# Block-diagonal centroid products, weight joins through PSUM and a re-ordered opening in a clustered-attention and MLP kernel

## The chip, the cores and the metric

The kernel runs on one core of a Trainium2 chip. A core has a matmul engine (TensorE, called PE in the profile; its weight loads are shown apart as PEld), a vector engine (DVE), an activation engine (ACT), a general engine (POOL) and a queue that issues most of the transfers (SP). Each of them executes its own instructions strictly in program order and waits on semaphores for the others. PE writes only to PSUM, in banks of 512 float32 values per partition; DVE and ACT read PSUM and SBUF. The metric is the device time of one execution in microseconds (us).

## The reference

For each of 4 batches and 8 heads, queries and keys (768 of them, 64 wide) are assigned to the nearest of 16 centroids of the head; a query attends only to keys of its own cluster. The result, laid out as 768 rows of 512, is mixed along the sequence by two thin matrices and goes through an MLP.

```python
q_assign = np.argmax(np.einsum('bhsd,hcd->bhsc', q_n, c_n), axis=-1)   # k_assign alike
mask = q_assign[:, :, :, None] == k_assign[:, :, None, :]
scores = np.where(mask, scale * np.matmul(q, k.transpose(0, 1, 3, 2)), -1000000000.0)
attn = np.exp(scores - np.max(scores, axis=-1, keepdims=True))
x = np.matmul(attn / (np.sum(attn, -1, keepdims=True) + 1e-09), v)     # heads side by side: 768 x 512
xt = x.transpose(0, 2, 1)
u = x + (xt @ U @ V).transpose(0, 2, 1)
out = u + np.maximum(u @ w_ch1, 0.0) @ w_ch2
```

Here q and k are the tensors themselves in the scores and q_n, k_n, c_n their normalised forms in the assignment. U, V and the two MLP weights arrive as float64.

## The kernel before

**Items.** The attention works on 16 items, each a pair of heads of one batch (index `i`, 4 items per batch). An item is loaded transposed into `R` (L303): queries on partitions 0-63, keys on 64-127, four blocks of 384 columns, one for each half of the sequence and each head. `sims` (L309) multiplies it with the turned centroids `cT` on PE, `largest` (L320) and `clusters` (L333) find the first largest of 16 on DVE (five operations) and leave a one-hot matrix `oh`. The one-hot rows are turned and scaled into rows 64-95 of the operand `X1`, so that the score product itself carries the mask: by `turn_clusters` (L399) for item 0, by `clusters_T` and `place_clusters` (transfers) for the others.

**Precision.** An operand is kept as a rounded part (`X1`, written by `split_hi`, ACT) and the rest (`X2`, written by `split_lo`, L360: POOL for the first two items, DVE for the others); transfers (`place_...`, queue SP) lay the two parts out in the buffer `arena` so that one pair of matmuls (L447, L449) gives the full score.

**Maxima, scores, values.** `rowmax` (L415) makes 24 products per item and half-row (L423), and DVE reduces each (L425) into `m2`; `rowmax_T` (L427) takes the larger of two halves (L430, `m`), and `rowmax_place` (L432) turns that on PE (L435), negates it on ACT (L437) and sends it by a transfer on ACT's queue to row 96 of `X2`. `scores` (L441) makes a tile `st`, ACT exponentiates it to `pr` (L452), `weights` (L455) adds the tiles up to `T` on POOL (a few on DVE), and `values` (L464) multiplies with V (L470, `o_ps`). `sums`, `sums_T` and `normalise` divide. `mix_u`, `mix_sum` and `mix_v` do the mixing for a batch.

**Weights.** They come as pairs of 32-bit words and are turned into float32 on the way: `upper` (L139, ACT) scales the high word into `rw_g`, and `join` (L147) puts shifted high bits, sign and low bits together in three DVE operations on the SBUF tile `rw_t` (L154, L156, L159), each issued as a stage of its own at its own time. `load_weights` (L165) then splits the result for four groups `g` of 8 pieces (ACT, and POOL or DVE); group 0 and three `mix` pieces lie inside the attention, group 1 around its end, groups 2 and 3 in the MLP. The MLP (`gemm1`, `gemm2`, L570 to L594) follows, all on PE, starting with `turn_u` (L561).

**What sets the order.** `at(time, fn, ...)` collects calls with a due time in units of one score tile (12 per item); the list is sorted by time and called in that order, and `keep_order` pins each engine to it. The due times are in `times`, `spots`, `start`, `mix` and `pieces`. All short-lived PSUM tiles come from one pool of four buffers (`work`, L124): a new tile waits until the readers of the tile four places earlier are done.

Of the kernel before, what the change touches and what calls it, by code (L numbers as in the profile page):

```python
# [29 lines left out]
F32 = mybir.dt.float32  # L30
F32R = mybir.dt.float32r
# [28 lines left out]
    "load0":           ( -34.7, -34.39, -42.04,   None,   None,  -24.6),  # L60
    "load1":           (-26.06, -29.53, -32.88,   None,   None, -24.08),
    "sims":            ( -25.1, -28.71, -28.37,   None,   None, -21.52),
    "clusters_T":      (-19.61, -19.11, -17.87,   None, -12.09, -14.53),
    "place_clusters":  (-18.66, -16.14, -16.18,   None, -10.54, -11.62),
    "split_hi0":       (-29.08, -30.53, -24.36,   None,   None, -21.63),
    "split_lo0":       (-24.34, -23.65, -24.04,   None,   None, -17.46),
    "split_hi1":       (-23.95,  -23.8, -24.91,   None,   None, -19.95),
    "split_lo1":       (-23.57, -19.94, -23.55,   None,   None, -17.17),
    "place_keys_hi":   (-20.26, -23.52, -23.41,   None,   None, -17.07),
    "place_keys_lo":   (-19.99, -19.89, -21.05,   None,   None, -16.87),  # L70
    "place_queries":   (-17.03, -15.79, -18.99,   None,   None, -16.31),
    "place_ones":      (-14.59, -12.48, -10.02,   None,   None, -19.67),
    "load_v":          (-19.47,  -3.83,  -5.91,   None, -22.04, -10.41),
    "rowmax":          (-14.88, -14.94,  -14.8, -13.95,  -8.61,  -11.6),
    "rowmax_T":        ( -3.08,  -3.31,  -3.73,  -2.67,  -0.09,  -1.59),
    "rowmax_place":    ( -2.26,  -2.27,   -2.6,    1.6,   2.02,  -0.01),
    "scores":          (     0,  -0.97,  -0.58,  -0.47,  -1.09,   0.95),
    "weights":         (  1.23,   0.08,   0.52,   2.09,   3.85,    1.7),
    "values":          (  1.27,   1.37,   0.22,   1.05,   3.05,   1.39),
    "sums":            ( 14.65,  14.41,  13.18,  14.01,  15.28,  15.65),  # L80
    "sums_T":          ( 16.16,  16.37,  14.51,  15.86,  17.12,   16.3),
    "normalise0":      ( 18.83,  16.88,  15.76,  22.66,  20.81,  21.01),
    "normalise1":      ( 21.68,  17.59,  15.29,  26.53,  23.24,  23.11),
    "largest":         (-23.05, -22.36, -20.51,   None,   None, -21.05),
    "clusters":        ( -21.3, -22.24, -19.87,   None,   None, -18.24),
# [3 lines left out]
spots = [0.61, 0.02, 1.8, 2.25, 1.26, 2.09, 2.97, 3, 3.58, 3.81, 4.64, 5.05]  # L89
# [13 lines left out]
def clustered_attention_moe(ctx: ExitStack, tc: tile.TileContext, qk, v, cen, moe_U, moe_V, w1, w2, out):  # L103
# [43 lines left out]
    def join(rw, g, t, k):  # L147
# [4 lines left out]
        if k == 0:  # L152
# [12 lines left out]
    def load_weights(g, step, stage):  # L165
# [39 lines left out]
    ident_b = one.tile([P, P], BF16, name="ident_b")  # L205
    make_identity(nc, ident_b)
    rank = one.tile([P, C], F32, name="rank")
    for c in range(C):
        nc.gpsimd.memset(rank[:, c:c + 1], float(C - c))
    osc = one.tile([P, 1], F32, name="osc")  # L210
    nc.gpsimd.memset(osc[0:64], 1.0)
    nc.gpsimd.memset(osc[64:128], BIG)
    obi = one.tile([P, 1], F32, name="obi")
    nc.gpsimd.memset(obi, 0.0)
# [6 lines left out]
    for g in range(4):
        for r in range(3):
            nc.gpsimd.tensor_copy(rep[32 * g:32 * g + 32, 32 * r:32 * r + 32],
                                  ident[32 * g:32 * g + 32, 32 * g:32 * g + 32])
# [17 lines left out]
    def turn_centroids(p):  # L244
        ps = work("ps_c")
        nc.tensor.transpose(ps[:, 0:P], c_sb[:, p], ident)
        for h in range(2):
            dst, src = (x.rearrange("p (s u c) -> p s u c", s=4, u=2)[:, :, h] for x in (cT[:, p, h], ps[:, 0:P]))
            nc.scalar.copy(dst, src)
# [20 lines left out]
    def load_mix(k, stage):  # L270
# [7 lines left out]
        elif stage < 5:  # L278
            parts["mix", k] = join(*parts["mix", k], stage - 2)
# [17 lines left out]
    live = {}  # L297

# [10 lines left out]
    def sims(i):  # L309

        ps = work("ps_sim")
        for h in range(2):
            for s in range(4):
                r = slice(64 * (s // 2), 64 * (s // 2) + 64)
                nc.tensor.matmul(ps[32 * s:32 * s + 32, 0:HS], cT[r, i % NP, h, 32 * s:32 * s + 32],  # L315
                                 live["R", i][r, 2 * h + s % 2, :], start=(h == 0), stop=(h == 1))
# [424 lines left out]
```

## Time and profile before

| | |
|---|---|
| three runs | 1041.81, 1037.4, 1041.7 us (median 1041.7) |
| the profiled execution | 1038.17 us; its span from first to last instruction is 1036.3 us, so 1.9 us lie around it |
| busy over the span | PE 999.4, PEld 793.5, DVE 533.2, ACT 350.1, POOL 342.6 us |
| opening, before the first score | 0 to 35.7 us |
| attention | 35.7 to about 479 us |
| MLP | about 479 to 1036.3 us |

A row of the time line gives start, duration, engine, line of the kernel, operation, output and inputs with their shapes, the number of instructions merged in the row, and in square brackets how long the engine had stood idle before it and what ended that. A row of the windows gives for a stretch of time the busy time of each engine, then the TensorE clock that was granted (1.00 is full), the share of the DMA engines and GB/s.

### The profile page before, as it was taken

The page shows a single profiled execution, that of the slowest core. Times are in us where ns is not written, and L with a number is a line of the kernel's source. Part 1 is how long each engine was busy: PE and PEld are TensorE (multiplying, and loading weights), DVE is VectorE, ACT ScalarE, POOL GpSimd, SP SyncE. Part 2 cuts the span into 40 slices and gives each one's busy share as a digit, 9 for nine tenths or more (in the row PEclk, how much of TensorE's full clock was granted, in tenths as well). Part 3 has the DMA queues.
Part 4 walks back from the last instruction along what each step waited for, and adds up shares of the span by engine and source line. Part 5 has one row for each costly group of instructions (what it writes and reads, how often), then busy time and mean ns, then how long its engine had stood idle before and what let it go on. Part 6 is the DMA issues. An engine that isn't in the chain of part 4 may idle for free.

```text
span 1036.3 us, 13926 instructions
## 1 busy us (share of the span) xinstructions
PE 999.4 (96%) x5496; PEld 793.5 (77%) x5496; DVE 533.2 (51%) x928; ACT 350.1 (34%) x572; POOL 342.6 (33%) x228
## 2 busy tenths in 40 slices
PE   4889999999999999989999999999999999999998
PEld 2566666666666666656889999999999999999997
DVE  4698898888898768798773121121121221211211
ACT  4344555555555544455332111111111111111110
POOL 4455667788578857754231000000000000000000
PEclk8799999999999999989999999999999999999999
DMA  5746453665565544243442001010010010100000
GB/s 147 192 119 150 132 150 93 198 158 144 128 196 140 140 97 129 71 129 103 151 164 80 1 1 61 1 38 24 1 62 1 1 61 1 61 1 1 31 1 31
DMA packets 28688, 87.73 MB, mean 85 GB/s; under 512 B 4880, under 2 KB 9488, under 8 KB 28112
## 3 DMA queue, kind: packets, MB, share of 16 engines
q1 hardware_dynamic: 28240, 86.76, 29.8%
q8 instruction: 43, 0.70, 0.3%
q14 instruction: 21, 0.17, 0.1%
q10 hardware_dynamic: 384, 0.10, 0.0%
HBM read 42.99 MB, written 12.58 MB: 54 GB/s over the span
## 4 chain that ended last, share of the span: by engine, by line
PE 87%; DVE 4%; ACT 1%; DMA 1%; issue 1%; ACTq 0%; DVEq 0%; SPq 0%
PE o_ps L470 12%; PE ps_h L576 9%; PE ps_h L578 9%; PE ps_h L577 9%; PE y L594 9%; PE y L593 9%; PE y L592 8%; PE ps_max L423 6%; PE st L447 6%; PE st L449 5%; PE ps_sim L315 1%; PE ps_sum L482 1%; DVE m L425 1%; PE ps_oT L503 1%; PE ps_uT L565 1%
## 5 line engine op out<-in xcount | busy, mean ns | idle before, releaser
L582 DVE SCALAR_TENSOR_TENSOR hl<-ps_h,hh 128x384 fp32r<-128x384 f32 x128 | 71.3, 557 | 349.6 <-ACT hh L581 349.6
L462 POOL TENSOR_TENSOR T<-T,pr 128x768 f32<-128x768 f32 x120 | 229.6, 1913 | 59.6 <-DVE T L462 26.7
L425 DVE TENSOR_REDUCE m<-ps_max 128x1 f32<-128x384 f32 x384 | 195.0, 547 | 58.7 <-PE ps_max L423 57.4
L581 ACT ACTIVATE hh<-ps_h 128x384 fp32r<-128x384 f32 x128 | 62.9, 492 | 375.5 <-PE ps_h L578 375.4
L452 ACT ACTIVATE pr<-st 128x768 f32<-128x768 f32 x192 | 155.3, 813 | 86.2 <-PE st L449 70.9
L423 PE MATMUL ps_max<-arena 128*128 128x384 f32 x384 | 125.3, 381 | 11.3 <-DVE oh L342 4.1
L470 PE MATMUL o_ps<-pr,vt 128*64 128x384 f32 x768 | 131.5, 492 | 0.0
L593 PE MATMUL y<-w2l,hh 128*128 128x512 f32 x288 | 113.6, 394 | 0.0
L447 PE MATMUL st<-arena 128*128 128x384 f32 x384 | 106.3, 358 | 2.3 <-ACT pr L452 2.3
L423 PEld LDWEIGHTS ps_max<-arena 128*128 128x128 f32 x384 | 71.2, 194 | 45.6 <-issue 16.1
L470 PEld LDWEIGHTS o_ps<-pr,vt 128*64 128x64 f32 x768 | 52.4, 137 | 65.8 <-issue 59.9
L449 PE MATMUL st<-arena 97*128 97x384 f32 x384 | 100.3, 343 | 1.3 <-DMA arena<-mT 1.3
L462 POOL TENSOR_TENSOR T<-pr 128x768 f32<-128x768 f32 x30 | 59.5, 1985 | 79.1 <-ACT pr L452 79.1
L447 PEld LDWEIGHTS st<-arena 128*128 128x128 f32 x384 | 67.2, 192 | 17.6 <-issue 9.9
L594 PE MATMUL y<-w2h,hl 128*128 128x512 f32 x192 | 76.1, 396 | 0.0
L594 PE MATMUL y<-arena,hl 128*128 128x512 f32 x192 | 75.9, 396 | 0.0
L592 PE MATMUL y<-w2h,hh 128*128 128x512 f32 x192 | 75.1, 391 | 0.0
L592 PE MATMUL y<-arena,hh 128*128 128x512 f32 x192 | 74.8, 390 | 0.0
L449 PEld LDWEIGHTS st<-arena 97*128 97x128 f32 x384 | 71.5, 192 | 2.0 <-DMA arena<-mT 1.9
L593 PEld LDWEIGHTS y<-w2l,hh 128*128 128x128 f32 x288 | 54.0, 188 | 9.1
L474 ACT COPY os<-o_ps 128x384 f32<-128x384 f32 x32 | 15.4, 480 | 99.9 <-PE o_ps L470 99.9
L576 PE MATMUL ps_h<-arena,w1h 128*128 128x384 f32 x128 | 44.7, 349 | 0.5 <-DVE arena L568 0.5
(130 smaller groups left out, 1634.2 us busy)
## 6 DMA issues: line engine op xcount, KB each, us to landing
rw<-in_w SPq DMA_DIRECT2D x32, 512.0 KB, 3.8
R<-in_qk SPq DMA_DIRECT2D x32, 384.0 KB, 5.2
arena<-arena SPq DMA_DIRECT2D x32, 384.0 KB, 3.6
arena<-arena SPq DMA_DIRECT2D x64, 192.0 KB, 2.8
vt<-in_v SPq DMA_DIRECT2D x16, 384.0 KB, 3.3
u_scr<-xt SPq DMA_DIRECT2D x4, 1536.0 KB, 5.4
u<-u_scr SPq DMA_DIRECT2D x8, 768.0 KB
out_y<-u SPq DMA_DIRECT2D x24, 256.0 KB, 2.0
```

Of the source, the lines that this page charges most:

```text
L423: nc.tensor.matmul(ps[:, 0:HS], x1[:, 0, g // 2, g % 2, t * P:(t + 1) * P], x1[:, 1, h, g % 2, :], start=True, stop=True)
L425: nc.vector.reduce_max(live["m2", i][:, h, u:u + 1], ps[:, 0:HS], axis=AX.X)
L447: nc.tensor.matmul(st[:, j, 0:HS], x1[:, 1, hk, j, ks], x1[:, 0, h, j, :], start=True, stop=False)
L449: nc.tensor.matmul(st[:, j, 0:HS], x2[0:97, 1, hk, j, ks], x2[0:97, 0, h, j, :], start=False, stop=True)
L452: nc.scalar.activation(pr, st[:, :, 0:HS], AF.Exp, scale=SCALE)
L462: eng.tensor_add(T, live["p", i, h, 0] if c == 1 else T, live["p", i, h, c])
L470: nc.tensor.matmul(o_ps[64 * j:64 * j + 64, 0:HS], vv[:, c, j, :], pr[:, j, :], start=(c == 0), stop=(c == NT - 1))
L576: nc.tensor.matmul(ps[:, 0:HS], w1h[:, d, fs], uh[:, d, :], start=(d == 0), stop=False)
L577: nc.tensor.matmul(ps[:, 0:HS], w1h[:, d, fs], ul[:, d, :], start=False, stop=False)
L592: nc.tensor.matmul(y[t], hh[:, ts], w2h[:, f % FG, :], start=(f == 0), stop=False)
L593: nc.tensor.matmul(y[t], hh[:, ts], w2l[:, f % FG, :], start=False, stop=False)
L594: nc.tensor.matmul(y[t], hl[:, ts], w2h[:, f % FG, :], start=False, stop=(f == NF - 1))
```

## The change

These edits belong together:

- `cT` holds for each head a 128x32 block-diagonal matrix (16 columns for the queries on partitions 0-63, 16 for the keys below), so that `sims` is four full-height products in place of eight half-height ones. The order of the one-hot tiles follows (`tile_of`), and `osc` and `obi` alternate by 32 rows in place of 64.
- `turn_clusters` is called by head `j` in place of by query or key; the first of its four copies is on DVE, the other three on ACT.
- For the first six maxima of item 0, `rowmax_place` makes six products of one column of `m` with the identity, which land as a row on partition 96 of PSUM; DVE and ACT negate one half each straight into `X2`. The transfer is gone there.
- `spin` puts transposes of the identity into an unused PSUM tile at ten places of the opening (40 in all).
- Joins of the weight groups 0 and 1 and of the mixing matrices are one stage: the two partial results go to a PSUM tile `ps_t`, and the third operation writes `rw_t` from it. Groups 2 and 3 stay as they were.
- `split_lo` of an item's second half is on POOL for all items.
- The constants are set in another order: `cT` (a quarter of its former size) first, what the opening needs next, `rep`, `sel` and the second one-hot buffer later.
- In the opening, `norms` of centroid pairs 1 to 3 comes ahead of the placing of the clusters in place of after it, and the maxima go in the order 0 to 5.
- `pr` has 11 buffers in place of 10.
- Due times move by up to a few units throughout.

```diff
+order0 = [-71, -70, -69, -65.96, -68.07, -66, -65.55, -64.02, -62.25, -62, -59.19, ...]
-    "rowmax":          (-14.88, -14.94,  -14.8, -13.95,  -8.61,  -11.6),
+    "rowmax":          (-14.88, -14.94,  -14.8, -12.18,  -8.11, -10.78),
...
+        if k is None:
+            b = work("ps_t").bitcast(I32)[0:r, 0:n]
+            t = raw.tile([P, 512], I32, name="rw_t")[0:r, 0:n]
+            nc.vector.tensor_scalar(b, g, 3, None, op0=ALU.logical_shift_left)
+            nc.vector.scalar_tensor_tensor(out=b, in0=g, scalar=-0x80000000, in1=b,
+                                           op0=ALU.bitwise_and, op1=ALU.bitwise_or)
+            nc.vector.scalar_tensor_tensor(out=t, in0=low, scalar=29, in1=b,
+                                           op0=ALU.logical_shift_right, op1=ALU.bitwise_or)
+        elif k == 0:
...
-            parts[g, step] = join(*parts[g, step], stage - 2)
+            if g > 1:
+                parts[g, step] = join(*parts[g, step], stage - 2)
+            elif stage == 3:
+                parts[g, step] = join(*parts[g, step], None)
...
-    cT = one.tile([P, NP, 2, P], F32, name="cT")
+    cT = one.tile([P, NP, 2, 2 * C], F32, name="cT")
...
-        for h in range(2):
-            dst, src = (x.rearrange("p (s u c) -> p s u c", s=4, u=2)[:, :, h] for x in (cT[:, p, h], ps[:, 0:P]))
-            nc.scalar.copy(dst, src)
+        for t in range(2):
+            r = slice(64 * t, 64 * t + 64)
+            nc.scalar.copy(cT[r, p, :, t * C:t * C + C],
+                           ps[r, 0:2 * P // 4].rearrange("p (j t c) -> p j t c", j=2, t=2)[:, :, t])
...
+    def spin(k, n):
+        ps = work("ps_spin")
+        for _ in range(n):
+            nc.tensor.transpose(ps[:, 0:P], ident, ident)
...
-        for h in range(2):
-            for s in range(4):
-                r = slice(64 * (s // 2), 64 * (s // 2) + 64)
-                nc.tensor.matmul(ps[32 * s:32 * s + 32, 0:HS], cT[r, i % NP, h, 32 * s:32 * s + 32],
-                                 live["R", i][r, 2 * h + s % 2, :], start=(h == 0), stop=(h == 1))
+        for s in range(4):
+            nc.tensor.matmul(ps[32 * s:32 * s + 32, 0:HS], cT[:, i % NP, s % 2], live["R", i][:, s, :],
+                             start=True, stop=True)
...
-        eng = nc.gpsimd if i < 2 else nc.vector
+        eng = nc.gpsimd if i < 2 or h == 1 else nc.vector
...
+        if i == 0 and u0 == 0:
+            m = live.pop(("m", i, u0))
+            for j in range(2):
+                ps = work("ps_mT")
+                for t in range(HT):
+                    nc.tensor.matmul(ps[96:97, t * P:(t + 1) * P], m[:, j * HT + t:j * HT + t + 1], ident,
+                                     start=True, stop=True)
+                dst = X2[0][96:97, 0, 0, j]
+                if j:
+                    nc.scalar.mul(dst, ps[96:97, 0:HS], -1.0)
+                else:
+                    nc.vector.tensor_scalar(dst, ps[96:97, 0:HS], -1.0, None, op0=ALU.mult)
+            return
```

The opening on DVE, before: the one-hot matrix of item 0 (`oh`), the two copies of the turned clusters into `arena`, the norms of centroid pairs 1 to 3 (128x192 and 128x3 results) and the twelve maxima with their last reduction.

```order
L342 TENSOR_TENSOR oh_153<-ps_simT,rank 128x12x2x16
L409 TENSOR_SCALAR arena<-st,osc,obi 32x2x384 x2
L256 TENSOR_TENSOR rw_g<-rw_g 128x192
L257 TENSOR_REDUCE c_n_149<-rw_g 128x3
L259 TENSOR_SCALAR c_n_148<-c_n_147 128x3
L260 RECIPROCAL c_rn<-c_n_148 128x3
L261 TENSOR_TENSOR c_rn<-c_rn,c_n_149 128x3
L262 TENSOR_TENSOR c_n_148<-c_n_148,c_rn 128x3
L263 TENSOR_SCALAR c_n_148<-c_n_148 128x3
L264 RECIPROCAL c_rn<-c_n_148 128x3
L425 TENSOR_REDUCE m_275<-ps_max 128x1 x12
L430 TENSOR_REDUCE m<-m_275 128x6
```

The same place on DVE with the change:

```order
L378 TENSOR_TENSOR oh_122<-ps_simT,rank 128x24x16
L294 TENSOR_TENSOR rw_g<-rw_g 128x192
L295 TENSOR_REDUCE c_n_130<-rw_g 128x3
L297 TENSOR_SCALAR c_n_129<-c_n_128 128x3
L298 RECIPROCAL c_rn<-c_n_129 128x3
L299 TENSOR_TENSOR c_rn<-c_rn,c_n_130 128x3
L300 TENSOR_TENSOR c_n_129<-c_n_129,c_rn 128x3
L301 TENSOR_SCALAR c_n_129<-c_n_129 128x3
L302 RECIPROCAL c_rn<-c_n_129 128x3
L452 TENSOR_SCALAR arena<-st,osc,obi 32x2x384
L464 TENSOR_REDUCE m_296<-ps_max 128x1 x12
L469 TENSOR_REDUCE m<-m_296 128x6
```

The norms moved ahead of the copy of the clusters, and one of the two copies left DVE. Some rows later, the negation of three maxima (L485) enters between the second and third operation of the search for item 1.

On PE, the end of the same stretch before: the products for the maxima of item 0, the transpose of the first six maxima (`ps_mT`), the transposes that feed item 1's search (`ps_simT`), the products for the other maxima and the first score.

```order
L423 MATMUL ps_max<-arena 128x384 x12
L435 MATMUL ps_mT<-ident,m 6x128
L325 MATMUL ps_simT<-ident,sims 128x128 x3
L423 MATMUL ps_max<-arena 128x384 x12
L447 MATMUL st<-arena 128x384 x2
```

And with the change:

```order
L462 MATMUL ps_max<-arena 128x384 x2
L336 MATMUL ps_spin<-ident 128x128 x4
L362 MATMUL ps_simT<-ident,sims 128x128 x3
L336 MATMUL ps_spin<-ident 128x128 x2
L479 MATMUL ps_mT<-ident,m 1x128 x6
L336 MATMUL ps_spin<-ident 128x128 x4
L462 MATMUL ps_max<-arena 128x384 x12
L500 MATMUL st<-arena 128x384 x2
```

The transposes for the search now stand ahead of the placing of the maxima, which wait for the reduction, where they stood behind it; idle products stand between.

At the end of the attention, DVE before, from the third-last stretch of reductions of the last item (`m_4474`) up to its maxima (`m`); `rw_t` rows are single operations of joins of weight group 1.

```order
L425 TENSOR_REDUCE m_4474<-ps_max 128x1 x2
L159 SCALAR_TENSOR_TENSOR rw_t<-rw,rw_t 128x512
L425 TENSOR_REDUCE m_4474<-ps_max 128x1
L504 TENSOR_TENSOR xt<-ps_oT,rv 128x3x128
L425 TENSOR_REDUCE m_4474<-ps_max 128x1 x2
L156 SCALAR_TENSOR_TENSOR rw_t<-rw_g,rw_t 128x512
L154 TENSOR_SCALAR rw_t<-rw_g 128x512
L425 TENSOR_REDUCE m_4474<-ps_max 128x1
L430 TENSOR_REDUCE m<-m_4474 128x12
```

And with the change:

```order
L464 TENSOR_REDUCE m_4481<-ps_max 128x1 x5
L174 TENSOR_SCALAR ps_t<-rw_g 128x512
L175 SCALAR_TENSOR_TENSOR ps_t<-rw_g,ps_t 128x512
L177 SCALAR_TENSOR_TENSOR rw_t<-rw,ps_t 128x512
L464 TENSOR_REDUCE m_4481<-ps_max 128x1
L557 TENSOR_TENSOR xt<-ps_oT,rv 128x3x128
L464 TENSOR_REDUCE m_4481<-ps_max 128x1 x3
L469 TENSOR_REDUCE m<-m_4481 128x12
```

Two whole joins (six operations, one shown) stand ahead of the last maxima in place of seven single operations, and no join operation stands between the last four reductions.

More of the change, by code (lines that the diff above doesn't have):

```diff
@@ L59 @@
 times = {
[L60 to L73, printed above, removed]
@@ new lines @@
+    "normalise0":      ( 18.83,  16.88,  14.88,   22.3,  20.85,  23.08),
+    "normalise1":      ( 21.59,  17.72,  15.28,  26.53,  23.84,  19.17),
+    "largest":         (-23.05, -22.46, -20.54,   None,   None, -21.24),
+    "clusters":        ( -21.3, -22.34, -20.12,   None,   None, -18.18),
+}
+mixes = {
+    "mix_u":    ( 18.88,  18.35,  18.81,  16.57),
+    "mix_sum":  ( 19.25,  19.13,   19.1,   18.6),
+    "mix_v":    (  20.5,   20.4,  20.66,  19.42),
+}
+stages = {
+    "mix":  (  4.41,   7.02,  11.43,  15.04,  16.45,  17.16),
+    "g0":   ( 35.66,  38.22,  41.05,  42.54,  42.54,  51.82),
+    "g1":   (-26.11, -21.73, -21.07,  -20.5,  -20.5, -18.35),
+    "g2":   ( -2.37,  -1.41,  -0.87,  -0.74,  -0.75,  -0.21),
+    "g3":   (  5.27,   6.49,   6.53,   7.36,   7.03,   8.06),
+}
@@ L202, in copy_rows @@
         queue.dma_start(out=dst.bitcast(F32), in_=src.bitcast(F32))
-    ident_b = one.tile([P, P], BF16, name="ident_b")
-    make_identity(nc, ident_b)
+    cT = one.tile([P, NP, 2, 2 * C], F32, name="cT")
+    nc.gpsimd.memset(cT, 0.0)
     rank = one.tile([P, C], F32, name="rank")
@@ L209, in clustered_attention_moe, with constants @@
         nc.gpsimd.memset(rank[:, c:c + 1], float(C - c))
+    ident_b = one.tile([P, P], BF16, name="ident_b")
     osc = one.tile([P, 1], F32, name="osc")
-    nc.gpsimd.memset(osc[0:64], 1.0)
-    nc.gpsimd.memset(osc[64:128], BIG)
     obi = one.tile([P, 1], F32, name="obi")
-    nc.gpsimd.memset(obi, 0.0)
-    nc.gpsimd.memset(obi[64:128], -BIG)
     sel = late.tile([P, 32], F32, name="sel")
-    nc.gpsimd.memset(sel, 0.0)
-    nc.gpsimd.memset(sel[:, 0:1], 1.0)
     rep = late.tile([P, 96], F32, name="rep")
[L221 to L224, printed above, removed]
-    cT = one.tile([P, NP, 2, P], F32, name="cT")
-    nc.gpsimd.memset(cT, 0.0)
+    onehot = [one.tile([P, NT, 4, 32], BF16, name=f"oh_{i}") for i in range(2)]
+    ones = one.tile([2 * NT, P], F32R, name="ones")
+    def constants(k):
+        if k == 0:
+            nc.gpsimd.memset(ones.bitcast(F32), 1.0)
+            nc.gpsimd.memset(onehot[0], 0.0)
+            make_identity(nc, ident_b)
+            for k in range(4):
+                nc.gpsimd.memset(osc[32 * k:32 * k + 32], (1.0, BIG)[k % 2])
+                nc.gpsimd.memset(obi[32 * k:32 * k + 32], (0.0, -BIG)[k % 2])
+        else:
+            nc.gpsimd.memset(onehot[1], 0.0)
+            nc.gpsimd.memset(sel, 0.0)
+            nc.gpsimd.memset(sel[:, 0:1], 1.0)
+            for g in range(4):
+                for r in range(3):
+                    nc.gpsimd.tensor_copy(rep[32 * g:32 * g + 32, 32 * r:32 * r + 32],
+                                          ident[32 * g:32 * g + 32, 32 * g:32 * g + 32])
     c_sb = raw.tile([P, 512], F32, name="rw_g").rearrange("p (n d) -> p n d", n=NP)
@@ L278, in load_mix @@
         elif stage < 5:
-            parts["mix", k] = join(*parts["mix", k], stage - 2)
+            if stage == 3:
+                parts["mix", k] = join(*parts["mix", k], None)
         else:
```

108 lines of the change are left out of this document (54 added, 54 removed).

## The prediction

> **What bounds the kernel now.** I read the page first, then the busy times by stage, then the waits and the time line of the opening and of the end of the attention.
>
> ```profile
> span 1036.3 us, 13926 instructions
> ...
> PE 999.4 (96%) x5496; PEld 793.5 (77%) x5496; DVE 533.2 (51%) x928; ACT 350.1 (34%) x572; POOL 342.6 (33%) x228
> ...
> PEclk8799999999999999989999999999999999999999
> ```
>
> PE is busy for 96% of the span, and the granted clock is below nine tenths in only three of the forty slices. The stages tell where it is not PE:
>
> ```profile
> 62.30:100.00 37.70, 33.61 (x195) 22.14 (x197) 32.47 (x61) 17.04 (x25) 22.72 (x12) 0.95 0.53 130
> 100.00:420.00 320.00, 317.69 (x1965) 213.66 (x1962) 264.99 (x474) 176.38 (x255) 230.96 (x124) 1.00 0.54 144
> 420.00:479.00 59.00, 51.08 (x278) 32.84 (x277) 48.65 (x64) 31.71 (x49) 38.55 (x21) 0.94 0.29 92
> 479.00:1037.00 558.00, 553.01 (x2821) 496.46 (x2821) 147.57 (x246) 97.96 (x196) 25.48 (x17) 1.00 0.11 38
> ```
>
> The columns behind the length are busy PE, PEld, DVE, ACT, POOL. From 100 to 420 PE is busy 99% and from 479 to the end of its work as well: there only fewer PE cycles shorten anything. From 420 to 479 PE idles 59.0 - 51.1 = 7.9 us while DVE is busy 82%. Before 36 us PE has little to do and a chain through DVE and ACT sets the pace. So the change is worth something in three places: the PE work of every item, the opening, and the end of the attention. The MLP (54% of the span) is issued as before apart from small shifts of weight loads that PE does not wait for; I cost these, and `pr`'s eleventh buffer, at nothing.
>
> **Term 1, the centroid products.** The chain of waits shows both shapes in one item, and the group row shows how many there are:
>
> ```profile
> 311.36 1.43 PE ps_sim L315 x16
> ...
> 321.75 0.78 PE ps_sum L482 x8
> ```
>
> ```profile
> L315 PE MATMUL ps_sim<-R,cT 64*32 64x384 f32 x256 | 25.2, 511 | 3.3 <-ACT cT L249 3.3
> ```
>
> 256 records are 16 for each of 16 items. Eight half-height products (two records each) take 1.43 us; `sums` issues four full-height products with 32 columns each and 384 moving columns, exactly what `sims` issues now, and takes 0.78. So an item saves 1.43 - 0.78 = 0.65 us of PE. Items 0 and 1 lie in the opening; the other 14 save 14 x 0.65 = 9.1 us on the engine that bounds. I take **9**.
>
> **Term 2, the opening.**
>
> ```profile
> 2.83 0.45 PE L246 MATMUL ps_c<-ident,rw_g 128*128 128x128 f32 x1 [2.83 <-POOL obi L214]
> ...
> 6.33 0.33 ACT L249 COPY cT<-ps_c 128x64 f32<-128x64 f32 x2 [4.10 <-POOL cT L229]
> ...
> 6.59 2.79 PE L315 MATMUL ps_sim<-R,cT 64*32 64x384 f32 x16 [3.31 <-ACT cT L249]
> ```
>
> The copies of `cT` waited 4.10 us for POOL's clearing of it. That clearing now comes first and is a quarter as long, so `cT` is there at about 2.83 + 0.45 + 0.33 = 3.6. When the queries and keys land isn't shown; they were there at 6.59. The products then took 2.79 us, about twice the 1.43 of later ones (a slow clock); halved they take 1.4. They end between 3.6 + 1.4 = 5.0 and 6.59 + 1.4 = 8.0, where they ended at 9.38: a gain between 1.4 and 4.4. Since four large transfers are in the queue by then, I stay near the late end: 2.5.
>
> ```profile
> 13.20 0.56 DVE L342 TENSOR_TENSOR oh<-ps_simT,rank 128x384 bf16<-128x384 f32 x1
> ...
> 15.32 0.98 ACT L412 ACTIVATE arena<-st,obi,osc 32x768 fp32r<-32x768 bf16 x1 [4.22 <-PE st L405]
> ...
> 18.22 1.07 DVE L409 TENSOR_SCALAR arena<-st,osc,obi 32x768 fp32r<-32x768 bf16 x1 [0.81 <-ACT arena L412]
> ...
> 19.32 0.36 DVE L256 TENSOR_TENSOR rw_g<-rw_g 128x192 f32<-128x192 f32 x1
> ...
> 21.35 0.18 DVE L264 RECIPROCAL c_rn<-c_n 128x3 f32<-128x3 f32 x1
> 21.56 5.66 DVE L425 TENSOR_REDUCE m<-ps_max 128x1 f32<-128x384 f32 x12
> 21.64 0.58 ACT L318 ACTIVATE sims<-ps_sim,c_rn 128x384 f32<-128x384 f32 x1 [1.33 <-DVE c_rn L264]
> ```
>
> DVE wrote the one-hot matrix until 13.76 and started the maxima at 21.56, 7.8 us later, after placing two cluster copies and the norms (19.32 to 21.53, 2.2 us). Now the norms run while PE turns the clusters, then one copy on DVE (1.07) and one on ACT (0.98) free the first two maxima at 2.2 + 1.1 + 1.0 = 4.3 us behind the one-hot matrix. The third needs the PSUM buffer of item 1's `ps_sim`, four places earlier, which ACT reads (0.58) behind four short copies and two more of 0.98: at 4.3 + 0.6 + 2.0 + 0.6 = 7.5, plus a product of 0.4. So ten maxima follow from 7.9 and end 4.7 later, at 12.6; before, the end was at 27.22 - 13.76 = 13.5. Gain 0.9.
>
> ```profile
> 28.53 0.56 DVE L329 TENSOR_REDUCE mx<-ps_simT 128x24 f32<-128x384 f32 x1 [1.11 <-PE ps_simT L325]
> ...
> 35.74 0.84 PE L447 MATMUL st<-arena 128*128 128x384 f32 x2
> ```
>
> DVE waited 1.11 us for `ps_simT`, which now stands ahead of the placing; the added negation of 384 values takes about 0.5 in its place, so 0.6. The transfer of the first maxima was not late: the first score at 35.74 comes behind the second twelve products for maxima, which follow DVE's pace, and in this stretch PE waits for no transfer. Placing those maxima by products saves nothing on the path. The sum is 2.5 + 0.9 + 0.6 = **4**, between 1.5 and 6.
>
> The idle products cost nothing while PE waits anyway. Whether they raise the clock, the time line and the windows (clock third from the end) tell:
>
> ```profile
> 13.82 1.46 PE L405 MATMUL st<-ident_b,oh 128*32 128x128 bf16 x12 [3.08 <-DVE oh L342]
> ...
> 15.83 1.28 PE L405 MATMUL st<-ident_b,oh 128*32 128x128 bf16 x12
> ```
>
> ```profile
> 16.40:16.80 0.40, 0.40 (x7) 0.40 (x5) 0.40 (x1) 0.40 (x4) 0.00 (x0) 0.51 0.53 115
> 16.80:17.20 0.40, 0.40 (x9) 0.29 (x11) 0.40 (x1) 0.08 (x1) 0.00 (x0) 1.00 1.04 269
> ```
>
> It rose from 0.51 to 1.00 at 16.8, after three busy microseconds in which PE ran transposes alone. The Trainium skill (TensorE: Matmul & The Clock Gate, Part 4: PE-mode transpose) says that transposes don't count as PE work for the clock; by that rule idle transposes would warm nothing, and this row speaks against it.
>
> **Term 3, the end of the attention.**
>
> ```profile
> PE ps_mT L435 <- DVE m L430: 4.1, 1, 4.1
> PE st L447 <- ACT pr L452: 2.3, 3, 1.3
> PE ps_max L423 <- DVE m L425: 1.7, 2, 1.3
> ```
>
> ```profile
> 301.99 4.02 PE o_ps L470 x24
> ```
>
> ```profile
> 444.76 2.03 DVE L154 TENSOR_SCALAR rw_t<-rw_g 128x512 int32<-128x512 int32 x1
> ...
> 448.20 0.99 PE L447 MATMUL st<-arena 128*128 128x384 f32 x2
> ...
> 452.38 4.72 PE L470 MATMUL o_ps<-pr,vt 128*64 128x384 f32 x24
> ```
>
> Busy DVE time in 425 to 480 of L154, L156 and L159, eight each:
>
> ```profile
> 425.00:480.00 55.00, 9.69 (x8) 0.94 0.31 99
> 425.00:480.00 55.00, 7.84 (x8) 0.94 0.31 99
> 425.00:480.00 55.00, 9.82 (x8) 0.94 0.31 99
> ```
>
> PE waits 4.1 us for the last item's maxima and 1.7 for other reductions, since DVE is in the joins of weight group 1: 27.35 us for eight, 3.4 each. How a join through PSUM runs isn't shown; the nearest rows are these:
>
> ```profile
> L154 DVE TENSOR_SCALAR rw_t<-rw_g x35: 250/428/2068, 62.2 to 548.2; 128x512 int32<-128x512 int32 x32, 96x384 int32<-96x384 int32 x2, 128x192 int32<-128x192 int32 x1
> L533 DVE TENSOR_TENSOR xt<-ps_h,xt x24: 673/679/693, 173.4 to 519.7; 128x512 f32<-128x512 f32 x24
> ```
>
> From SBUF to SBUF the same operation takes 0.43 or 2.07 us (minimum, median and maximum are shown in ns); one that has a PSUM operand takes 0.68 every time, also while POOL adds. So a join costs 3 x 0.68 = 2.0 (bounds: 1.3 at the undisturbed SBUF times, 3.4 as now) and eight save 11 us of DVE. The Trainium skill (VectorE: DVE Perf Modes, Why PSUM operands drop a tier) says that a PSUM operand excludes the doubled float32 rate; by it alone the first operation would lose 0.25 us against 0.43. The rows show this loss, and that the spread it replaces is larger.
>
> Ahead of the last maxima stood seven join operations (7 x 3.4 / 3 = 8.0 us), now six (4.1): 3.9 us earlier, against waits of 5.8. The wait of 4.1 also cost clock: `o_ps` behind it took 4.72 for what takes 4.02 elsewhere, and three score tiles (twelve products) stand in 448.2 to 452.4, 4.2 us, half of it lost at half pace: 2.8 in all. Of these, and of 2.3 us behind ACT, I take 2.6, since PE and DVE now share four PSUM buffers with the joins. Sum **6.5**, between 0 and 10.9.
>
> **Other terms at nothing.** POOL takes over 14 half rests:
>
> ```profile
> L363 DVE TENSOR_TENSOR arena<-R,arena 128x768 fp32r<-128x768 f32 x28 | 42.5, 1521 | 0.1
> L363 POOL TENSOR_TENSOR arena<-R,arena 128x768 fp32r<-128x768 f32 x4 | 7.2, 1810 | 13.2 <-ACT arena L358 13.1
> ```
>
> That is 25 us more on POOL, 21 less on DVE. In 100 to 420 POOL goes from 231 of 320 to some 254 of 312, 81%: the additions behind a rest are served late, but not short of time.
>
> **Sum.** 9 + 4 + 6.5 = 19.5 us off the profiled execution's 1038.2 (span and 1.9 around it): 1018.7, so 1019. That execution lies 3.5 under the median of 1041.7 and 0.8 above the lowest run; if the changed kernel's runs scatter alike, its median may come out up to 3.5 higher, which the range covers.
>
> **Rivals.** (1) *The end of the attention keeps its stalls*: the joins are faster, but `o_ps` now waits for a join's PSUM buffer, or the rounding on ACT and the weight transfers behind it set the pace. For: PE already waits 2.3 us on ACT there. Against: DVE was the busiest. Term 3 is lost: 1025. (2) *The idle products warm nothing*: then the six products that place the maxima and the first eight score products run at half pace; from the row at 35.74 I estimate 0.1 us lost on each, 1.4: 1020. The rows at 16.8 speak against it. This is the case of the clock rule cited above. (3) *Slower, by the four PSUM buffers*: the tile four places behind a join can be written only when DVE has finished it. If DVE comes to each of the 19 joins late, PE stands for up to a join's length: 19 x 2.0 = 38, giving 1057. It decides from 19.5 / 19 = 1.0 us a join. Against: in the program's order most joins of group 0 are issued behind an `o_ps`, whose 4.02 us leave DVE without new maxima, and the tile four places ahead of a join, for which DVE itself waits, is never an `o_ps`. (4) *POOL becomes the bound*, for rests that wait with the additions queued behind them; term 1 and half of term 3 are lost: 1031.
>
> **How the numbers follow.** Forecast 60% (1019; its own range 1011 to 1026), rival 1 20%, rival 2 9%, rival 3 5%, rival 4 6%. The range 1009 to 1031 takes in rivals 1, 2 and 4 and nearly all of the unknown costs (the low ends of terms 2 and 3 give 1028, the high ends 1012, and some more for the ramp at 62 to 100). A difference of 0.5%, 5 us, is about what a measurement of this kernel can tell from none. Faster 0.92, no change 0.03, slower 0.05.
>
> **What would show it.** `ps_sim` at 0.8 us an item; the first score at about 31.7; joins at 2.0 with little spread; no wait of `ps_mT` for `m` near 440; the MLP as long as before. I am wrong if a `ps_t` holds up DVE or PE, or if PE idles in 100 to 420.

## The result and the profile after

The changed kernel takes 1023.17 us in the median of four runs (1022.46 to 1025.6), the kernel before 1041.26 in the median of four beside them; the ratio is 0.984, with a 95% interval of 0.981 to 0.987. The predicted 1019 lies 4 us under it, inside the range of 1009 to 1031. The profiled execution took 1025.6 us, the slowest of the four.

The page of the changed kernel, first its span, then the busy times and the granted clock in forty slices:

```profile
span 1023.5 us, 13820 instructions
...
PE 999.9 (98%) x5419; PEld 796.3 (78%) x5419; DVE 488.9 (48%) x914; ACT 350.6 (34%) x573; POOL 361.8 (35%) x246
...
PEclk9999999999999999989999999999999999999999
```

DVE has lost 44 us of work and POOL gained 19. PE's busy time has hardly changed (999.4 before): against the 9.4 us that the centroid products have lost (25.2 before, 15.8 now) stand, in the main, 9.2 us of idle products. One slice is below nine tenths of the clock, where three were. So the time must be looked for by stretches. The windows of the changed kernel, divided at the first score, at the start of the fifth and of the 28th `o_ps` and at the first `ps_uT` (columns as in the prediction):

```profile
0.00:33.68 33.68, 26.84 (x126) 17.36 (x127) 20.57 (x51) 12.42 (x24) 13.34 (x54) 0.94 0.69 179
33.68:105.10 71.42, 66.22 (x374) 45.35 (x373) 55.89 (x109) 37.87 (x56) 45.91 (x25) 0.96 0.54 136
105.10:412.43 307.33, 304.67 (x1837) 207.23 (x1837) 229.16 (x453) 172.57 (x252) 242.76 (x132) 1.00 0.55 148
412.43:466.57 54.14, 49.26 (x264) 29.76 (x264) 38.05 (x61) 29.23 (x47) 34.01 (x20) 0.94 0.31 101
466.57:1024.00 557.43, 552.92 (x2823) 496.62 (x2821) 145.18 (x245) 98.49 (x196) 25.75 (x17) 1.00 0.11 38
```

Set beside the same events in the kernel before, and in a second profiled execution of the changed kernel (the run e1 below, 1022.44 us):

| stretch | before, us | changed, us (gain) | e1, us (gain) |
|---|---|---|---|
| start to first score | 35.74 | 33.68 (2.1) | 32.34 (3.4) |
| to the fifth `o_ps` | 72.31 | 71.42 (0.9) | 70.21 (2.1) |
| to the 28th `o_ps` | 314.44 | 307.33 (7.1) | 308.18 (6.3) |
| to the first `ps_uT` | 56.42 | 54.14 (2.3) | 52.79 (3.6) |
| to the end of the span | 557.4 | 556.9 (0.5) | 557.1 (0.3) |
| span | 1036.3 | 1023.5 (12.8) | 1020.6 (15.7) |

The centroid products, which stand in every item, show as predicted in the chain of waits: one item's eight records take what `sums` takes.

```profile
303.28 0.78 PE ps_sim L352 x8
...
313.40 0.78 PE ps_sum L535 x8
```

The three operations of a join, by line, with minimum, median and maximum in ns, are each about 0.69 us in the common shape:

```profile
L174 DVE TENSOR_SCALAR ps_t<-rw_g x19: 348/681/687, 69.5 to 459.2; 128x512 int32<-128x512 int32 x16, 96x384 int32<-96x384 int32 x2, 128x192 int32<-128x192 int32 x1
L175 DVE SCALAR_TENSOR_TENSOR ps_t<-rw_g,ps_t x19: 362/696/697, 69.9 to 459.9; 128x512 int32<-128x512 int32 x16, 96x384 int32<-96x384 int32 x2, 128x192 int32<-128x192 int32 x1
L177 DVE SCALAR_TENSOR_TENSOR rw_t<-rw,ps_t x19: 353/686/689, 70.3 to 460.7; 128x512 int32<-128x512 int32 x16, 96x384 int32<-96x384 int32 x2, 128x192 int32<-128x192 int32 x1
```

The end of the attention is where the forecast missed most. Its time line, by engine:

```profile
433.45 0.28 PE L488 MATMUL ps_mT<-ident,m 128*12 128x128 f32 x1 [0.16 <-DVE m L469]
...
435.18 0.25 ACT L490 ACTIVATE mT<-ps_mT 12x128 fp32r<-12x128 f32 x1
435.46 0.73 ACTq L232 DMA_DIRECT2D arena<-mT  x1
...
437.16 0.62 PE L500 MATMUL st<-arena 128*128 128x384 f32 x2 [1.41 <-ACT pr L505]
439.75 0.98 PE L502 MATMUL st<-arena 97*128 97x384 f32 x2 [1.97 <-DMA arena<-mT]
440.65 6.77 PE L523 MATMUL o_ps<-pr,vt 128*64 128x384 f32 x24
```

The wait of `ps_mT` for the last maxima has shrunk from 4.13 to 0.16 us. But ACT, with a rounding, an exponential and a weight copy ahead, turns to the row only 1.7 us later, the transfer lands some 4 us after that, and PE stands for it in the last item's first score tile. PE's wait of 1.41 us just before, for an exponential, belongs to it: by the trace that exponential stood behind ACT's issuing of the transfer (0.73 us) and an addition on POOL. The window from 435 to 440 has PE busy for 1.62 us, and in the next five the clock is half:

```profile
435.00:440.00 5.00, 1.62 (x7) 1.02 (x7) 4.93 (x7) 3.00 (x6) 4.84 (x3) 0.93 0.33 108
440.00:445.00 5.00, 5.00 (x16) 1.94 (x18) 2.83 (x4) 0.94 (x2) 2.45 (x2) 0.50 0.90 299
```

### The profile page after: what moved, and what is told of

Read it like the earlier page. It is cut to its first block, busy times and chain, and to the rows that moved or that the text cites. A ratio compares the mean times of both kernels' runs of the same rounds, so it can differ in the third digit from the quotient of the medians.

```text
span 1023.5 us, 13820 instructions
## 1 busy us (share of the span) xinstructions
PE 999.9 (98%) x5419; PEld 796.3 (78%) x5419; DVE 488.9 (48%) x914; ACT 350.6 (34%) x573; POOL 361.8 (35%) x246
## 4 chain that ended last, share of the span: by engine, by line
PE 90%; DVE 5%; ACT 1%; issue 1%; DMA 1%; POOL 1%; ACTq 0%; SPq 0%; DVEq 0%; POOLq 0%
PE o_ps L523 12%; PE ps_h L629 9%; PE ps_h L631 9%; PE ps_h L630 9%; PE y L647 9%; PE y L646 9%; PE y L645 9%; PE ps_max L462 7%; PE st L500 6%; PE st L502 6%; DVE m L464 2%; PE ps_sim L352 1%; PE ps_sum L535 1%; PE ps_uT L618 1%; PE ps_oT L556 1%
## 5 line engine op out<-in xcount | busy, mean ns | idle before, releaser
L515 POOL TENSOR_TENSOR T<-T,pr 128x768 f32<-128x768 f32 x120 | 228.1, 1901 | 48.9 <-ACT pr L505 20.5
L523 PE MATMUL o_ps<-pr,vt 128*64 128x384 f32 x768 | 133.7, 499 | 0.0
L515 POOL TENSOR_TENSOR T<-pr 128x768 f32<-128x768 f32 x30 | 56.4, 1881 | 60.7 <-ACT pr L505 60.7
```

Of the source, the lines that this page charges most:

```text
L515: eng.tensor_add(T, live["p", i, h, 0] if c == 1 else T, live["p", i, h, c])
L523: nc.tensor.matmul(o_ps[64 * j:64 * j + 64, 0:HS], vv[:, c, j, :], pr[:, j, :], start=(c == 0), stop=(c == NT - 1))
```

## The experiments

All are timed in five rounds against the kernel before; "ratio" is to that. One ten-thousandth is 0.1 us. Times of the first four stand beside each other in one session on one chip, so their medians are compared directly; the others by their ratios.

**e1: the changed kernel again.** No edit.

> The changed kernel once more, as the reference for the runs beside it: a ratio of 0.984 (0.981 to 0.987) to the kernel before. If its end of the attention loses time as a rule and not in one execution, its trace shows again a wait of about 2.0 us of the score product L502 for the transfer of the row of maxima near 440, and an o_ps behind it that takes 6.8 instead of 4.0 us at a lower clock; if that was chance, the o_ps takes about 4.0.

1023.95 us, ratio 0.9838 [0.9825, 0.9851]. The stall is a rule: 1.42 us for ACT, 2.00 for the row, and an `o_ps` of 5.74.

**e2: centroid products of half height.**

```diff
-            nc.tensor.matmul(ps[32 * s:32 * s + 32, 0:HS], cT[:, i % NP, s % 2], live["R", i][:, s, :],
-                             start=True, stop=True)
+            for k in range(2):
+                r = slice(64 * (s // 2), 64 * (s // 2) + 64)
+                nc.tensor.matmul(ps[32 * s:32 * s + 32, 0:HS], cT[r, i % NP, s % 2], live["R", i][r, s, :],
+                                 start=(k == 0), stop=(k == 1))
```

> The changed kernel with each centroid product issued as two products of half height (64 rows, the same 64 rows twice), so 16 records an item instead of 8; one half of each sum is left out, so the clusters come from part of the similarities. Theory (term 1: these products stand on the bounding engine in 14 items, 0.65 us each): 9 us slower than the changed kernel, with up to 2 more for items 0 and 1 in the opening, so 8 to 11. Rival (other engines set the pace of the items, PE's share only fills): under 3 us.

1034.53 us, 10.6 over e1, inside the 8 to 11 of the theory. The window of the tile `ps_sim` in e1 between the fifth and the 28th `o_ps` (eleven items; the first column behind the length is PE):

```profile
102.00:411.00 309.00, 9.38 (x88) 1.73 (x88) 6.37 (x11) 1.00 0.55 147
```

The same of e2:

```profile
108.00:423.00 315.00, 16.65 (x176) 5.15 (x176) 6.39 (x11) 1.00 0.54 144
```

That is 16.65 - 9.38 = 7.3 us more PE work, 0.66 an item, and this stretch is 315.13 - 308.18 = 7.0 us longer. Work on the bounding engine comes back in the time one for one.

**e3: joins in SBUF again, still one step.**

```diff
-            b = work("ps_t").bitcast(I32)[0:r, 0:n]
-            t = raw.tile([P, 512], I32, name="rw_t")[0:r, 0:n]
+            t = b = raw.tile([P, 512], I32, name="rw_t")[0:r, 0:n]
```

> The changed kernel with the joins of the mixing weights and of groups 0 and 1 in SBUF again, in the same single step and at the same places. Theory (term 3: the time of a join decides when the last item's maxima are done): joins at 3.4 us instead of 2.06, ps_mT waits for m near 433 by 2 to 4 us, and the time is 2 to 5 us longer. Rival A (the place of the steps did it, not the operand): within 1 us. Rival B (through PSUM costs PE its buffers): 1 to 2 us faster.

1036.75 us, ratio 0.9966 [0.9954, 0.9979]: 12.8 us over e1, more than twice what the theory allowed. Of the 14.1 us between the two traces 1.4 lie in the opening, ahead of any join, 3.6 from the first score to the fifth `o_ps`, 0.7 from there to the 28th and 8.1 behind it. One join in e3's time line, with POOL's additions beside it, and another when POOL has stopped:

```profile
424.51 7.95 POOL L514 TENSOR_TENSOR T<-T,pr 128x768 f32<-128x768 f32 x4
...
426.68 1.92 DVE L173 TENSOR_SCALAR rw_t<-rw_g 128x512 int32<-128x512 int32 x1
428.63 2.18 DVE L174 SCALAR_TENSOR_TENSOR rw_t<-rw_g,rw_t 128x512 int32<-128x512 int32 x1
430.84 2.17 DVE L176 SCALAR_TENSOR_TENSOR rw_t<-rw,rw_t 128x512 int32<-128x512 int32 x1
...
433.54 0.69 PE L461 MATMUL ps_max<-arena 128*128 128x384 f32 x1 [5.36 <-DVE m L463]
434.15 5.95 PE L522 MATMUL o_ps<-pr,vt 128*64 128x384 f32 x24
...
435.26 0.41 DVE L173 TENSOR_SCALAR rw_t<-rw_g 128x512 int32<-128x512 int32 x1
435.71 0.69 DVE L174 SCALAR_TENSOR_TENSOR rw_t<-rw_g,rw_t 128x512 int32<-128x512 int32 x1
436.43 0.69 DVE L176 SCALAR_TENSOR_TENSOR rw_t<-rw,rw_t 128x512 int32<-128x512 int32 x1
```

And the same join through PSUM in the changed kernel, again beside additions:

```profile
420.54 7.59 POOL L515 TENSOR_TENSOR T<-T,pr 128x768 f32<-128x768 f32 x4
...
422.69 0.68 DVE L174 TENSOR_SCALAR ps_t<-rw_g 128x512 int32<-128x512 int32 x1
...
423.40 0.70 DVE L175 SCALAR_TENSOR_TENSOR ps_t<-rw_g,ps_t 128x512 int32<-128x512 int32 x1
...
424.19 0.69 DVE L177 SCALAR_TENSOR_TENSOR rw_t<-rw,ps_t 128x512 int32<-128x512 int32 x1
...
424.93 0.91 PE L462 MATMUL ps_max<-arena 128*128 128x384 f32 x2 [0.92 <-DVE rw_t L177]
```

Beside additions a join in SBUF takes 6.3 us, one operation to about one addition (7.95 / 4 = 2.0); without them 1.8; through PSUM 2.1 either way. In e3 PE waited 5.36 us for the reductions queued behind the join (at `ps_max`; `ps_mT`, where the theory looked for the wait, waited 0.16); in the changed kernel it waited 0.92 us at the same place, for the PSUM buffer of the join itself. The longer gap brought a slow `o_ps` (5.95) as well. The Trainium skill (SBUF — State Buffer, Who interferes with whom) gives a rule that fits: a DVE operation with two SBUF inputs, or one in a doubled mode, shares a port pair with POOL and is shut out while a POOL operation that reads SBUF holds it, whereas one with at most one SBUF input outside those modes isn't. Every operation of the new join is of the latter kind, and the rows agree.

**e4: the last item's first score tile behind `o_ps`.**

```diff
-            at(when("scores", i) + k, scores, i, h, c)
+            at(max(when("scores", i) + k, NS * i + 0.5 if i == n - 1 else -1e9), scores, i, h, c)
```

> The changed kernel with one thing moved: the last item's first score tile is issued behind the o_ps of the item before it instead of ahead of it. Theory (what ate most of term 3 is a new wait: the score product stands for the transfer of the row of maxima, 1.97 us, ahead of it 1.41 for ACT, and the clock falls in that gap, so that o_ps takes 6.77 instead of 4.02): the transfer lies beside o_ps, and the time is 3 to 6 us shorter. Rival (ACT's queue, the joins on DVE or the additions on POOL set this stage anyway, and the wait moves to the next tile): within 1.5 us.

1019.21 us, ratio 0.9793 [0.9780, 0.9805]: 4.7 us under e1. Its time line shows the row of maxima travelling beside `o_ps`, which now runs at full speed:

```profile
434.98 4.09 PE L523 MATMUL o_ps<-pr,vt 128*64 128x384 f32 x24
439.00 0.62 PE L500 MATMUL st<-arena 128*128 128x384 f32 x2
440.31 0.59 PE L502 MATMUL st<-arena 97*128 97x384 f32 x2 [0.69 <-DMA arena<-mT]
```

So the new wait cost the changed kernel almost 5 us, and what is left of it there is 0.69 us.

**e5: no idle products.**

```diff
     for k, (fn, *args) in enumerate(start):
-        at(order0[k], fn, *args)
+        if fn is not spin:
+            at(order0[k], fn, *args)
```

> The changed kernel without its idle products (the ten groups of transposes of the identity), whose PSUM buffers leave the ring with them. Theory (idle transposes raise the clock): the granted clock in 10 to 36 is lower than with them (0.97 and 0.86 in 10 to 20 and 20 to 30), the products for the first maxima run at half pace, and the time is 1 to 3 us longer. Rival (they warm nothing, or what they warm isn't on the path): within 0.7 us, or up to 1 us shorter, since the products for the maxima no longer queue behind them.

Ratio 0.9833 [0.9819, 0.9848]: no difference to e1. Rows of the opening of e1, PE alone:

```profile
4.90 1.72 PE L352 MATMUL ps_sim<-R,cT 128*32 128x384 f32 x8
7.30 0.55 PE L362 MATMUL ps_simT<-ident,sims 128*128 128x128 f32 x3 [0.68 <-ACT sims L355]
...
11.04 0.84 PE L444 MATMUL st<-ident_b,oh 128*32 128x128 bf16 x12 [1.99 <-DVE oh L378]
...
18.75 1.01 PE L462 MATMUL ps_max<-arena 128*128 128x384 f32 x2 [2.18 <-ACT sims L355]
...
32.34 0.79 PE L500 MATMUL st<-arena 128*128 128x384 f32 x2
```

And of e5:

```profile
4.53 2.42 PE L352 MATMUL ps_sim<-R,cT 128*32 128x384 f32 x8 [1.18 <-DMA R<-in_qk]
7.62 0.90 PE L362 MATMUL ps_simT<-ident,sims 128*128 128x128 f32 x3 [0.68 <-ACT sims L355]
...
11.71 1.46 PE L444 MATMUL st<-ident_b,oh 128*32 128x128 bf16 x12 [2.98 <-DVE oh L378]
...
16.33 0.85 PE L462 MATMUL ps_max<-arena 128*128 128x384 f32 x3
19.35 3.67 PE L462 MATMUL ps_max<-arena 128*128 128x384 f32 x9 [2.17 <-ACT sims L355]
...
32.18 0.84 PE L500 MATMUL st<-arena 128*128 128x384 f32 x2
```

Neither theory is quite right. With idle products `sims` and the two groups of transposes are 0.7, 0.35 and 0.6 us shorter, and before these `sims` PE had run transposes alone. The twelve transposes took 0.84 us in ten of the eleven profiled executions with idle products (1.46 in the first one of the changed kernel) and 1.46 in all three without (before, e5 and e9). So idle transposes do raise the clock, though not in every execution. By the rule weighed in the prediction (the Trainium skill, TensorE: Matmul & The Clock Gate, Part 4: PE-mode transpose) the times would be alike with and without them; the rows disagree with it. The sign that the theory named did not come: the clock column of e5 reads 0.98 and 0.84 in 10 to 20 and 20 to 30, as good as the 0.97 and 0.86 of the changed kernel. But it reads 1.00 for e5 at 11.71 too, where the transposes run at half pace, so in the opening the durations are the better witness.

The first score still comes no earlier with idle products, and the rows of the maxima show where the gain goes. An idle tile takes one of the four PSUM buffers as well: in e1 the third product for a maximum has to wait for the buffer that item 1's scaling frees (18.75), in e5 only the fourth (19.35). Behind that wait DVE has ten reductions left in e1 (5.01 us, done at 24.49) and nine in e5 (4.28 us, done at 24.14).

**e6: the first maxima placed by a transfer again.**

```diff
-        if i == 0 and u0 == 0:
+        if False:
```

> The changed kernel with the first six tiles' maxima placed by one transpose and a transfer again, as the kernel before does, in place of twelve products and two negations. Theory of the prediction (the transfer isn't late, so placing by products saves nothing): within 0.7 us, or 0.5 shorter for the negation of 0.56 us that leaves DVE. Rival (the first score waits for the transfer): 1 to 3 us longer.

Ratio 0.9838 [0.9822, 0.9853], as e1: the twelve products buy nothing.

**e7: the rests of all second halves on DVE from item 2 on.**

```diff
-        eng = nc.gpsimd if i < 2 or h == 1 else nc.vector
+        eng = nc.gpsimd if i < 2 else nc.vector
```

> The changed kernel with the second half of the rests (items 2 to 15) on DVE again, 14 of about 1.5 us, instead of POOL. Theory of the prediction (no stage's end hangs on it): within 1 us; PE stays 99% busy in 100 to 410. Rival (DVE's room is what keeps PE supplied): waits of ps_max for m come up, 2 to 5 us longer.

Ratio 0.9857 [0.9839, 0.9874], about 2 us over e1, between the two theories. The intervals overlap, but all four of its times (from 1024.91 us on) lie above all eight of e5 and e6 in the same session (up to 1024.76), so some loss is likely. In the trace it stands before 95 us: from the second to the fourth `o_ps` 37.6 us where e1 took 34.4, while the stretch to the 28th is as long (308.2). Part of this is not the edit's: the first execution of the changed kernel took 36.0 there as well, with a fall of the clock near 90 like that of e7.

**e8: item 1's scaling ahead of the second pair of cluster copies.**

```diff
-        at(order0[k], fn, *args)
+        at(-39.5 if (fn, *args) == (turn_clusters, 0, 1) else order0[k], fn, *args)
```

> The changed kernel with item 1's centroid products and their scaling on ACT issued ahead of the second pair of cluster copies instead of behind it. Theory (the third product for a maximum stands 2.2 us for the PSUM buffer that this scaling frees; the second pair of clusters is wanted from the seventh maximum on only): that wait goes, the first score comes 1.5 to 2.2 us earlier, and the time is as much shorter. Rival (the seventh maximum now waits for the copies, or the maxima's pace on DVE sets the opening): 0 to 0.7 us.

Ratio 0.9819 [0.9803, 0.9835], 2.0 us under e1 as the theory had it, though the intervals overlap. In the time line of the changed kernel the third product for a maximum waited 2.17 us for the PSUM buffer:

```profile
19.90 1.01 PE L462 MATMUL ps_max<-arena 128*128 128x384 f32 x2 [2.17 <-ACT sims L355]
```

In that of e8 it waits 0.17, and the first score comes at 30.50, where it came at 31.88 to 33.78 in six profiled executions with the opening unmoved (the changed kernel, e1, e3, e4, e7 and e10):

```profile
17.04 0.81 PE L462 MATMUL ps_max<-arena 128*128 128x384 f32 x2 [0.17 <-ACT sims L355]
...
30.50 0.51 PE L500 MATMUL st<-arena 128*128 128x384 f32 x2
```

**e9: joins through PSUM alone, in the kernel before.** `join` gets the branch of the change, and is called once, in the place where the second of the three operations stood (the mixing weights alike):

```diff
...
-            parts[g, step] = join(*parts[g, step], stage - 2)
+            if g > 1:
+                parts[g, step] = join(*parts[g, step], stage - 2)
+            elif stage == 3:
+                parts[g, step] = join(*parts[g, step], None)
```

> The kernel before with the joins through PSUM alone: the mixing weights and groups 0 and 1 join in one step at the place where the second of the three operations stood. Theory (term 3: a join's time on DVE holds up PE, and the joins alone bring this): joins at 2.06 us instead of 3.4, the wait of ps_mT for m near 447 gone, 3 to 8 us faster than the kernel before. Rival (without the rest of the change the last item's row or ACT sets the stage as soon as DVE doesn't): within 2 us of the kernel before.

1042.23 us, ratio 1.0021 [1.0008, 1.0034]. The theory failed: what costs 12.8 us when taken out of the changed kernel brings nothing when put into the old one alone, and rather 2 us the other way. The time line of its end of the attention says why:

```profile
442.94 0.69 DVE L158 SCALAR_TENSOR_TENSOR rw_t<-rw,ps_t 128x512 int32<-128x512 int32 x1
...
444.36 0.28 PE L447 MATMUL ps_mT<-ident,m 128*12 128x128 f32 x1 [2.13 <-DVE m L442]
...
447.98 0.66 ACT L144 ACTIVATE rw_g<-rw 128x512 f32<-128x512 f32 x1 [3.00 <-DMA rw<-in_w]
448.55 0.25 ACT L449 ACTIVATE mT<-ps_mT 12x128 fp32r<-12x128 f32 x1
...
450.56 1.01 PE L459 MATMUL st<-arena 128*128 128x384 f32 x2 [4.17 <-ACT pr L464]
```

The maxima are ready 3 us earlier than in the kernel before (the wait for them is 2.13 us, not gone), but on ACT the row stands behind a copy (L144) that waits 3.00 us for the transfer of the next raw weights. That transfer needs the buffer `rw` of an earlier piece, free once the operation that takes its low words is done. Here that is the third of the step, due at -19.06 in units of a tile, and one starts at 442.94; in the kernel before (L159) it was due at -20.53 and started at 440.01. So the single step sits too late at this place; in the change it is due at -20.5. Whether the earlier place alone would mend it was not tried.

**e10: joins in SBUF and in three steps, at the new due times** (the mixing weights alike).

```diff
...
-            if g > 1:
-                parts[g, step] = join(*parts[g, step], stage - 2)
-            elif stage == 3:
-                parts[g, step] = join(*parts[g, step], None)
+            parts[g, step] = join(*parts[g, step], stage - 2)
```

> The changed kernel with the joins in SBUF and again as three separate steps, due at the times that its tables still hold for them. Theory (of the 12.8 us that SBUF joins in one step cost, a part comes from the three operations standing together, since a reduction that PE waits for then stands behind all of them): 3 to 7 us faster than that run, a ratio of 0.989 to 0.994. Rival (the operand alone makes the price): a ratio of 0.996 to 0.998 as in that run.

1039.22 us, ratio 0.9992 [0.9981, 1.0003], slower still than e3: a miss. It hides two effects of opposite sign. The end of the attention is 2.2 us shorter than in e3 (58.7 against 60.9), as the theory has it, but the stretch from the fifth to the 28th `o_ps` is 5.2 us longer (314.1 against 308.9): there PE waits 5.8 us for reductions, 1.8 in e3. So what made e3 dear is in the main not that the three operations stand together.

**e11: the moves of e4 and e8 together.** **e12: the same, with the first three groups of idle products alone**, by one more line:

```diff
...
+        if fn is not spin or args[0] < 3:
...
```

> The changed kernel with both moves: item 1's scaling ahead of the second pair of cluster copies, and the last item's first score tile behind o_ps. Theory (the two stalls stand in stages with nothing between them but work that PE bounds): the gains of 4.7 and 1.9 us add, a ratio of 0.977 to 0.978. Rival (the earlier start is lost in a later wait): a ratio of 0.979 to 0.981.

> As the kernel with both moves, with only the first three groups of idle products kept, and none between the products for maxima. Theory (the early ones shorten the first centroid products from 2.4 to 1.7 us and the transposes behind them; the later ones stand ahead of products that DVE waits for, whose nine then took 4.6 us where they take 3.7 without): 0.5 to 1.5 us faster than with all of them. Rival (DVE's reductions set that stretch, or the clock falls without them): within 0.4 us, or slower by up to 1.

e11: 1018.07 us, ratio 0.9782 [0.9762, 0.9803]; e12: 1016.84 us, 0.9781 [0.9760, 0.9802]. The best of all, some 6 us under the changed kernel. Whether the two gains add in full (0.9774) the interval can't tell; both stretches are short in the trace of e11 (first score at 30.97, end of the attention 48.2 us). That e12 gains 0.5 us or more over e11 isn't borne out, and its first score comes at 31.10: idle products between the products for maxima cost nothing that the opening feels.

## Why the prediction was right, and where its terms were off

**What bounds the kernel.** Right: PE idles in the opening, in the ramp behind it (62 to 100) and at the end of the attention, as before, and the stretch from the fifth to the 28th `o_ps` shrank by its PE work alone. The MLP is as long as before within 0.5 us.

**Term 1 (9).** Right. 7.1 and 6.3 us come in the eleven items between the marks (0.65 x 11 = 7.2); the other three items lie before the fifth `o_ps`. e2 shows it by taking it away.

**Term 2 (4).** The mechanism was right, the sizes only in part: the first score came at 33.68 and, in e1, at 32.34, not at 31.7. That is a gain of 2.1 and 3.4, and the six executions named under e8 give 2.0 to 3.9. Of the 2.5 for an earlier one-hot matrix the profiled execution has 13.76 - 12.21 = 1.55: `sims` started at 5.09, inside the bounds, but its eight records took 2.40 us at the low clock, not 1.4, and the transposes behind them 0.90 where they had taken 0.55. In e1, where the clock rose earlier, it has 13.76 - 10.99 = 2.8. The 0.9 for earlier maxima is lost: the first twelve reductions end 25.64 - 12.21 = 13.4 us behind the one-hot matrix, 13.5 before, since the third product came half a microsecond later than I had reckoned and the ten reductions took 5.01 us in place of 4.7. e8 shows that this buffer is the lever. Of the 0.6 there came 0.5: the second twelve reductions start 29.34 - 25.64 = 3.7 us behind the first, 31.40 - 27.22 = 4.2 before. That placing by products saves nothing is borne out by e6.

**Term 3 (6.5).** This is the step that was mis-sized: 2.3 and 3.6 us, inside the bounds of 0 to 10.9. Its first half held: a join takes 2.06 us with no spread, and the wait for the last maxima is gone. The step "3.9 us earlier, against waits of 5.8", with the clock's 2.8 on top, left out what stands between the maxima and PE: ACT's queue, then the transfer of the row. They became a wait of 3.4 us in two pieces, and the clock fell again, as it had before. Of rival 1 this is ACT's part; the transfer that PE waited for is that of the row, which rival 1 had not named, and `o_ps` waited for no join's buffer. My argument against rival 1, that DVE was the busiest, went by busy time (48.65 us of DVE against 31.71 of ACT in 420 to 479), which doesn't tell the wait that ends last; PE, at 51.08, was busier than either. e4 confirms the new wait by an order alone: 4.7 us, somewhat more than term 3 lacked.

**The joins elsewhere.** I costed joins outside the last stage at nothing but a little for the ramp. By e3 they are worth 2.4 to 3.6 us there in the new schedule: from the first score to the fifth `o_ps` e3 takes 73.8, the changed kernel 71.4 and 70.2. Yet in the changed kernel's traces this stretch gains only 0.9 and 2.1, in which term 1 has its three items (2.0). Both hold at once if the new times put joins where PE soon waits for DVE, which only the short join bears; e9 and e10 agree with this, since neither the joins nor the due times bring the gain alone, but how much belongs to which stays open.

**The terms at nothing.** Idle products: nothing on the path, as predicted (e5). Of what rival 2 put at stake, the products that place the maxima ran at full pace with and without the idle ones (1.47 us for twelve in the changed kernel and in e5; 2.72 in e12), but the first score products ran at half pace in both (0.84 us for two at 33.68 and, in e5, at 32.18, against 0.51 later). The idle products did not prevent that. POOL's 14 half rests: no cost, and perhaps a gain of up to 2 us that I did not see (e7). POOL did not become the bound, nor did the four PSUM buffers. My sign of being wrong, that a `ps_t` holds up DVE or PE, did come, but at a small size: PE waits twice for a join's last operation, 0.9 and 0.6 us in both traces.

**The sum.** 19.5 us were predicted off a profiled execution; one profiled execution gained 12.8, the other 15.7, and the medians differ by 18.1 (16.6 in the session of e1), since the profiled execution of before was among its kernel's faster and that of the change the slowest of its own. Judged by the stretches, term 2 lacks 0.6 to 1.9 and term 3 lacks 3 to 4. By the time itself, 1023.17, the forecast of 1019 is 4 us low, about what term 3 lacked; that the medians' gain of 18.1 comes so near to 19.5 is in part luck, since a term of which about half or less came met a starting execution faster than most.

## What to carry to other kernels

When a wait on one engine is removed, follow the result on to the engine that bounds, through each in-order queue and transfer on the way, and put a long piece of bounding work beside that path: here one tile's place was worth 4.7 us, more than the whole change had gained in that stage (2.3 and 3.6). Taking a part out of a change that was timed together with its order measures what the part is worth in the new order, not its share of the gain: e2 and e3 alone add up to 10.6 + 12.8 = 23.4 us, and the whole change brings 16.6 beside them. A DVE operation that is slow only beside another engine's work should be priced beside that work.

## What the runs showed of the hardware

The same SBUF operation took 0.41 us alone and 1.92 beside POOL's additions, and two with a second SBUF input 0.69 and 2.18, each about until one addition had ended; with an intermediate in PSUM all three took 0.68 to 0.70 both times. I had expected a spread, not that every operation of a join could be caught. A gap in which PE was busy for 1.62 of 5 us was followed by half clock (0.50) for five more, so a wait of 3.4 us cost another 2.7 in the `o_ps` behind it (6.77 in place of 4.09; 5.74 in e1, behind a wait as long).
